# Sigmoid attention and a token MLP: the first q load in two parts, the first three score steps on 256 and 192 queries, group 1's k cast by VectorE

## The chip, the cores and the metric

The kernel runs on one core of a Trainium2 chip. The core has five engines with a queue each, worked in order: TensorE (PE; its weight loads are shown apart as PEld), VectorE (DVE), ScalarE (ACT), GpSimd (POOL) and SyncE (SP), which here issues loads and stores. The transfers themselves run on 16 DMA engines. Matmul results land in PSUM, eight banks of 128 x 512 float32; all else is in SBUF. The metric is the device time of one execution in microseconds (us), lower being better.

## The reference

For 8 batches (u), 12 heads, 448 tokens and 64 values per head, all in float32:

```python
scores = scale * np.matmul(q, k.transpose(0, 1, 3, 2)) - np.log(S)
attn = 1.0 / (1.0 + np.exp(-scores))
x = np.matmul(attn, v)              # then heads side by side: (8, 448, 768)
wq, wk = x @ w_q, x @ w_k           # 768 -> 64
W_tok = scale * np.einsum('bsd,btd->bst', wq, wk)
mixed = np.einsum('bst,btd->bsd', W_tok, x)
out = np.maximum(mixed, 0.0) @ w_out
```

The attention is a sigmoid, so there is no row maximum and no sum to wait for: each block of scores becomes weights by one activation.

## The kernel before, in words

**Groups.** Four heads of one batch are a group; there are 24 groups (u, j). A group's q, k and v come as one load each of 128 x 896 float32 (`load1`, L165): partitions hold two heads by 64 rows, the free dimension holds the other two heads (g) by seven token blocks (i) by 64 values. Each is cast to bf16 (`cast1`, L188; GpSimd unless named otherwise).

**Transposes.** Scores need q and k with the head's 64 values on partitions. For groups 0 to 3, TensorE transposes all of q and k of a group into one PSUM pair (two banks), and one copy moves both to the tile `qk` (`tr`, L267 and L272). Group 4 and many later ones are cast into another layout (L178) and transposed by VectorE (L242, L218).

**Steps.** A group has seven score steps, one for each block of 64 keys (`scores`). A step takes a PSUM pair, makes four 64 x 64 matmuls of all 448 queries (L284), and ScalarE turns 128 x 896 scores to bf16 weights with the sigmoid (L289). Its pair is free when that activation is done. Steps are counted through: step 7 is the first of group 1, step 24 the fourth of group 3. `values` (L302) multiplies the weights with v; after seven steps the sum is copied to `xt` (L311). Then follow transposes of x (L325, L342), the MLP's matmuls (L368, L412, L452 and others) and the output projection (L497, L577), whose results are stored.

**What sets the order.** The string `PLAN` gives the order of the work on TensorE, one letter per piece: S a score step, q and k the transposes of the next group, P or p a values step, F a filler matmul of zeros, K (before only) the second part of group 0's k, other letters the rest. Other engines follow, since their instructions are emitted with the piece that needs them. PSUM pairs are handed out in turn from a list of four, `free2`. A filler writes to the pair that is next in that list. `ORDER` gives the order of loads; a point marks a cast by VectorE. The tiles `ld` for loads are six, so `pump_loads` issues a load once the tile six places before has been cast: SP waits for that cast. `cast_one` lets VectorE's casts be emitted `LAG` = 9 steps after their load.

**The start.** q of group 0 is loaded whole (L637), k in two parts (blocks 0 to 2, L638; 3 to 6, L639). During the first loads TensorE makes 32 matmuls of zeros (L650). VectorE casts blocks 0 to 3 of q, ScalarE 4 to 6, GpSimd both parts of k (L747). `tr_part` transposes one part into a pair and copies it to `qk[0]` (L758): q by VectorE and ScalarE, k by VectorE. Steps 0 and 1 follow, then the second k part, steps 2 to 4, group 1's q transposes, step 5, its k transposes, step 6, step 7. The end of `qk[1]`'s copy (L272) lets step 7 begin.

Of the kernel before, what the change touches and what calls it, by code (L numbers as in the profile page):

```python
# [10 lines left out]
BF16 = mybir.dt.bfloat16  # L11
# [6 lines left out]
def kernel(  # L18
# [12 lines left out]
    nc = tc.nc  # L31
# [4 lines left out]
    P = 128  # L36
# [35 lines left out]
    def bank2():  # L72
        n = free2.pop(0)
        return n, pairs[n], pairs16[n]
# [35 lines left out]
    def xt(u, j):  # L110
# [4 lines left out]


    PLAN = (
        "FFSSFKSFSSqFSkFSFSpFSpSqpPpPSPSSkFSpPSFSSabSrPSPSPXSsPSPpPSp"
        "pPpSPSXSwwSSzWWXwWSPPpSPppNSPSqkSXSSpUSPSpMpSPpPSqkSSPSpPMSP"
        "PPPSSWWXSSwWWWSPpcPSdMpSPPPSXSNSxSqkSUSpPSMppSppPSOoSMSOOqSk"  # L120
        "SoOSMrPpSppPSPSPOoSSsSOzXOSCLlLSLSLLSpPPPPcpPSSdOOSOSCNxSOSc"
        "USPPSPdprPSPPSPPsPPPSpSOPSXoSxSzooSCMLlCSLllLSPcpPSPPPPSCSOd"
        "XSSOOoSMpcpSPPPPSPSONSMYOxSpPpSpSCoodSpPPSoOSxSUSLcldllSLLPS"
        "PpSPpcpPdSoSOMSoSOSXmMrPsSpPPSPoSpOSPoSoozxSoScOSSOOOSOdNSOS"
        "USPppSMPpppPPPSpLPlSLLeppSflLOomgcOMooNOSxSoOStoSSOooeSpPdPP"
        "oPSpSPooSOfSooSSgPOoMpppSPPPOmMOSOSOSLLLlLSLSOoSOxScoOxSoSOO"
        "NdPPSPPPPSSPoOSOSOSooSxoSOSTPpSPPSPppPPMPPypMpPlLMLLyLLIxiiN"
        "IIuiIMiImmIIIOooOOOOoOOoooooo"
    )
    PLAN = "".join(PLAN)  # L130
    KIND = ["a"] + [t for t in PLAN if t in "qacer"]
# [102 lines left out]
    def tr(n, nm, kind):  # L234
        t = "qk".index(nm)
        if kind == "s":
            return
        if kind == "r":
            qk[n] = p_qk.tile([P, 2, 2, NI, NP], BF16, tag="qk", name="qk")
            w = pq[n].rearrange("p e t i d y -> p e (t i d y)").bitcast(F32)  # L240
            for e in range(2):
                nc.vector.transpose(out=qk[n][:, e].rearrange("p t i n -> p (t i n)").bitcast(F32), in_=w[:, e])  # L242
# [12 lines left out]
        t16 = ld.pop((nm + "16", n))  # L255
        if t == 0:
            ps_qk[n] = bank2()
        fb, _, ps = ps_qk[n]
        if kind in "abh":
            transposes_whole(ps[:, t], t16, slice(0, NI))  # L260
        else:
            transposes(ps[:, :, t * S : (t + 1) * S], t16, slice(0, NI))
        if t == 1:
            qk[n] = p_qk.tile([P, 2, 2, NI, NP], BF16, tag="qk", name="qk")
            copy = COPY["s" if kind in "jh" else "v"]
            if kind in "abh":
                copy(  # L267
                    out=qk[n].rearrange("p h t i n -> p t i h n"),
                    in_=ps[:, :, 0 : 2 * S].rearrange("p t (i h n) -> p t i h n", i=NI, h=2),
                )  # L270
            else:
                copy(  # L272
                    out=qk[n].rearrange("p h t i n -> p t h (i n)"),
                    in_=ps[:, :, 0 : 2 * S].rearrange("p h (t x) -> p t h x", t=2),
                )
            release(fb)

    ats = {}

    def scores(n, i):  # L280
        fb, sc, _ = bank2()
# [373 lines left out]


    ORDER = (
# [71 lines left out]

    def cast_one(e):  # L730
        todo = BY[e]
        if not (todo and todo[0] in issued and done["S"] >= issued[todo[0]] + LAG and ready(*todo[0])):
# [8 lines left out]
        while cast_one("s") or cast_one("v"):  # L741
            pass

    q016 = p_c16.tile([P, NI, 2, HD], BF16, tag="q16", name="q16")
    k016 = p_c16.tile([P, NI, 2, HD], BF16, tag="k16", name="k16")
    for t16, t32, r, e in ((q016, q0, IA, "v"), (q016, q0, IB, "s"), (k016, k0, KA, "g"), (k016, k0, KB, "g")):
        COPY[e](  # L747
            out=t16[:, r].rearrange("p i b d -> p b i d"),
            in_=t32[:, :, cols(r)].rearrange("p b (i d) -> p b i d", d=HD),
        )  # L750
    cast |= {("q", 0), ("k", 0)}
    pump_loads()
    qk[0] = p_qk.tile([P, 2, 2, NI, NP], BF16, tag="qk", name="qk")

    def tr_part(nm, t16, r, e):
        fb, _, ps = bank2()
        transposes_whole(ps[:, 0], t16, r)
        COPY[e](  # L758
            out=qk[0][:, :, "qk".index(nm), r].rearrange("p h i n -> p i h n"),
            in_=ps[:, 0, 0 : (r.stop - r.start) * P].rearrange("p (i h n) -> p i h n", h=2, n=NP),  # L760
        )
        release(fb)

    tr_part("q", q016, IA, "v")
    tr_part("q", q016, IB, "s")
    tr_part("k", k016, KA, "v")
# [7 lines left out]
    for t in PLAN:  # L774
# [29 lines left out]
        elif t == "z":  # L804
# [1 line left out]
            quadrants(n, 1)  # L806
            used.update({("q", n), ("k", n)})
            pump()
        elif t == "K":
            tr_part("k", k016, KB, "v")  # L810
        elif kind == "x":
            tr_x(c, tail, t in "XY", "s" if t in "yY" else "v")
        elif kind == "W":
# [58 lines left out]
```

## Time and profile before

| | |
|---|---|
| runs timed | 188.56, 190.07, 192.9 us (median 190.07) |
| the profiled execution | 188.87 us, of which the span of the trace is 186.8 us |
| granted TensorE clock, mean over the span | 0.996 |
| first sigmoid activation starts | 6.36 us |
| step 7's activation (first of group 1) starts | 12.90 us |
| ScalarE busy, 12 to 30 us | 17.96 of 18.00 us |
| TensorE busy, 12 to 30 us, by the model of the trace | 15.62 of 18.00 us |
| DMA engines' mean busy share, 12 to 30 us | 0.96, at 328 GB/s |

All times in the profile count from the start of the span. The profile is of one execution; the timed runs aren't profiled. A line of it names an engine, a source line of the kernel, an operation and the tiles (written <- read); "idle before <- releaser" tells how long the engine stood still and what ended that. Matmul ends are modelled, so that a busy TensorE isn't TensorE at its peak.

### The profile page before, as it was taken

How to read it: one execution, taken by the hardware profiler on the slowest of the kernel's cores; microseconds unless marked ns; L12 is line 12 of the kernel's file. 1: busy time of each engine (PE TensorE's matmuls, PEld its weight loads, DVE VectorE, ACT ScalarE, POOL GpSimd, SP SyncE). 2: the span in 40 equal slices, each digit the busy share in tenths (PEclk: the TensorE clock that was granted, in tenths of full speed). 3: DMA queues.
4: the chain of work that ended last, by engine and by line, in shares of the span. 5: the costliest groups of instructions: out<-in, count | busy, mean ns of one | idle time of the engine just before them, and what ended most of it. 6: DMA issues, size and time to landing. Idle time of an engine off the chain costs nothing.

```text
span 186.8 us, 8517 instructions
## 1 busy us (share of the span) xinstructions
PE 175.1 (94%) x3653; PEld 115.8 (62%) x3656; DVE 139.1 (74%) x211; ACT 163.8 (88%) x210; POOL 107.5 (58%) x145
## 2 busy tenths in 40 slices
PE   7778899989999999999999999999999999999990
PEld 7234556554555554565555776767998889786670
DVE  3234597677878999989898999979768565797810
ACT  4799999999999989999999999998999989975130
POOL 1454886894979989899999885387023820010000
PEclk9999999999999999999999999999999999999998
DMA  5998999985699989999999996994799733603485
GB/s 170 345 375 297 274 373 375 386 307 191 186 344 402 402 296 332 295 321 301 258 260 321 317 408 237 266 321 118 207 346 320 184 93 88 160 19 85 102 238 169
DMA packets 26389, 48.97 MB, mean 262 GB/s; under 512 B 4080, under 2 KB 20208, under 8 KB 26352
## 3 DMA queue, kind: packets, MB, share of 16 engines
q1 hardware_dynamic: 25952, 47.65, 78.2%
q10 hardware_dynamic: 400, 0.79, 1.2%
q8 instruction: 28, 0.46, 1.0%
q14 instruction: 9, 0.07, 0.1%
HBM read 35.78 MB, written 11.01 MB: 251 GB/s over the span
## 4 chain that ended last, share of the span: by engine, by line
PE 66%; DVE 14%; DMA 8%; ACT 4%; issue 3%; POOL 2%; SPq 1%; ACTq 0%; DVEq 0%; POOLq 0%
PE banks L284 14%; PE banks L302 13%; PE banks L497 13%; PE banks L577 10%; DMA q<-in_q_dram 4%; DVE qk L218 4%; DMA k<-in_k_dram 4%; DVE xt L311 3%; PE banks L534 3%; ACT at L289 3%; PE banks L368 3%; PE banks L412 3%; PE banks L342 2%; DVE mx L440 2%; PE banks L325 2%
## 5 line engine op out<-in xcount | busy, mean ns | idle before, releaser
L289 ACT ACTIVATE at<-banks 128x896 bf16<-128x896 f32 x168 | 141.8, 927 | 4.8 <-PE banks L284 3.4
L284 PE MATMUL banks<-qk 64*64 64x448 bf16 x672 | 62.8, 359 | 3.5 <-DVE qk L272 0.9
L302 PE MATMUL banks<-at,v 64*64 64x448 bf16 x672 | 46.6, 350 | 0.2
L284 PEld LDWEIGHTS <-qk 64*64 64x64 bf16 x672 | 25.8, 105 | 24.6 <-issue 14.2
L497 PE MATMUL banks<-wout,mx 64*64 64x384 bf16 x672 | 35.1, 323 | 0.0
L188 POOL CAST v<-v 128x896 bf16<-128x896 f32 x22 | 20.4, 931 | 17.6 <-DMA v<-in_v_dram 14.0
L302 PEld LDWEIGHTS <-v 64*64 64x64 bf16 x672 | 23.1, 106 | 7.8 <-issue 1.7
L497 PEld LDWEIGHTS <-mx 64*64 64x64 bf16 x672 | 24.2, 107 | 3.5
L440 DVE TENSOR_SCALAR mx<-banks 128x1024 bf16<-128x1024 f32 (+2 forms) x21 | 21.1, 1010 | 5.3 <-PE banks L464 3.0
L311 DVE CAST xt<-banks 128x896 bf16<-128x896 f32 x20 | 21.6, 1083 | 4.5 <-PE banks L302 2.6
L577 PE MATMUL banks<-wout,mx 128*128 128x384 bf16 (+1 forms) x138 | 24.7, 320 | 0.0
L577 PEld LDWEIGHTS <-mx 128*128 128x128 bf16 x138 | 11.9, 98 | 10.4 <-issue 4.5
L178 POOL CAST qk<-q 128x896 bf16<-128x896 f32 x13 | 15.5, 1196 | 2.7 <-DMA q<-in_q_dram 1.3
L178 POOL CAST qk<-k 128x896 bf16<-128x896 f32 x11 | 13.4, 1217 | 6.4 <-DVE qk L249 5.2
L249 DVE STREAM_TRANSPOSE qk<-qk 128x448 f32<-128x448 f32 x24 | 14.9, 629 | 0.0
L377 POOL COPY wq<-wqk 64x448 bf16<-64x448 bf16 x6 | 3.7, 619 | 16.9 <-DVE wqk L376 16.6
L153 POOL COPY qk<-swap 32x448 uint32<-32x448 uint32 x20 | 11.9, 593 | 1.2
L147 POOL COPY swap<-qk 32x448 uint32<-32x448 uint32 x20 | 11.1, 554 | 1.8 <-DVE qk L178 0.7
L506 DVE COPY o<-banks 128x768 f32<-128x768 f32 x9 | 8.6, 953 | 4.6 <-PE banks L497 4.6
L150 POOL COPY qk<-qk 32x448 uint32<-32x448 uint32 x20 | 11.1, 554 | 1.2
L606 ACT COPY o<-banks 128x384 f32<-128x384 f32 x10 | 4.8, 485 | 7.1 <-PE banks L577 4.9
L218 DVE STREAM_TRANSPOSE qk<-qk 32x448 f32<-32x448 f32 x16 | 10.2, 636 | 0.4
(91 smaller groups left out, 228.4 us busy)
## 6 DMA issues: line engine op xcount, KB each, us to landing
q<-in_q_dram SPq DMA_DIRECT2D x24, 448.0 KB, 6.2
v<-in_v_dram SPq DMA_DIRECT2D x24, 448.0 KB, 6.4
k<-in_k_dram SPq DMA_DIRECT2D x23, 448.0 KB, 6.1
out_dram<-o SPq DMA_DIRECT2D x51, 192.0 KB, 4.1
w<-in_moe_w_out_dram SPq DMA_DIRECT2D x6, 384.0 KB, 4.8
wout<-wout SPq DMA_DIRECT2D x12, 96.0 KB, 5.6
out_dram<-o ACTq DMA_DIRECT2D x3, 192.0 KB, 3.2
qk<-mv SPq DMA_DIRECT2D x8, 56.0 KB, 3.0
```

The costliest lines, as they stand in the source:

```text
L153: eng.tensor_copy(out=w[lo, 1], in_=z[lo])
L178: COPY[e](out=f[:, :, "qk".index(nm)].rearrange("p e i d y -> p e y i d"), in_=ld.pop((nm, n)).rearrange("p (y i e d) -> p e y i d", y=2, ...
L188: COPY[e](out=t16.rearrange("p i b d -> p b i d"), in_=ld.pop((nm, n)).rearrange("p b (i d) -> p b i d", i=NI),)
L218: nc.vector.transpose(out=qk[n][other : other + 32, h].rearrange("p t i n -> p (t i n)").bitcast(F32), in_=w[own : own + 32, 1 - h],)
L249: nc.vector.transpose(out=qk[n][:, t].rearrange("p t i n -> p (t i n)").bitcast(F32), in_=w)
L284: nc.tensor.matmul(sc[HALF[h], g, 0:S], qk[n][HALF[g], h, 1, i, :], qk[n][HALF[g], h, 0].rearrange("p i n -> p (i n)"), start=True, stop=True,
L289: nc.scalar.activation(at, sc[:, :, 0:S], ACTF.Sigmoid, bias=attn_bias, scale=attn_scale)
L302: nc.tensor.matmul(ps[HALF[g], h, 0:S], ld["v16", n][HALF[h], i, g, :], ats[n, i][HALF[h], g, :], start=(i == 0), stop=(i == NI - 1),)
L311: COPY[eng](out=xt(u, j)[:, :, 0:S], in_=ps[:, :, 0:S])
L440: nc.vector.tensor_scalar(dst, ps, moe_scale, 0.0, ALU.mult, ALU.max)
L497: nc.tensor.matmul(ps[HALF[x], y, 0:NB], mx[HALF[y], u, b, 64 * (i - 3 * y) : 64 * (i - 3 * y) + 64], wout16[HALF[y], slot(y, b), x * NB : ...
L577: nc.tensor.matmul(ps, mxs[w][:, 2 * S * c + m * P : 2 * S * c + (m + 1) * P], wout16[:, c, w0:w1], start=(c == 0), stop=(c == NC - 1),)
```

## The change

1. q of group 0 is loaded in two parts: blocks 0 to 3, then (behind k's first part) blocks 4 to 6.
2. Casts and transposes of group 0 are cut finer: q in three parts (0-1 VectorE, 2-3 ScalarE, 4-6 VectorE), k in four (block 0 and 1-2 GpSimd, 3-4 VectorE, 5-6 GpSimd). The copies of ScalarE's q part stay with ScalarE, all others go to VectorE.
3. Steps 0 to 2 are each done in two parts, 256 queries and then 192 (`scores_part`), with an activation for each part. All three keep their PSUM pair until the second part is done.
4. 23 matmuls of zeros come first, not 32, and three small fillers of 128 columns stand between the parts (`filler`).
5. Group 1's k is cast by VectorE (the point ahead of `k1` in `ORDER`, and no `LAG` for it), and its q and k are copied out of PSUM one by one, each as soon as it is transposed.
6. `PLAN` begins after step 2: step 6 stands ahead of group 1's k transposes, where it was behind them. The rest is as it was.

```diff
     PLAN = (
-        "FFSSFKSFSSqFSkFSFSpFSpSqpPpPSPSSkFSpPSFSSabSrPSPSPXSsPSPpPSp"
+        "FSSqFSFSkFSpFSpSqpPpPSPSSkFSpPSFSSabSrPSPSPXSsPSPpPSppPpSPSX"
...
@@ tr
+        if n == 1:
+            if t == 0:
+                qk[n] = p_qk.tile([P, 2, 2, NI, NP], BF16, tag="qk", name="qk")
+            nc.vector.tensor_copy(
+                out=qk[n][:, :, t].rearrange("p h i n -> p h (i n)"), in_=ps[:, :, t * S : (t + 1) * S],
+            )
+            if t == 1:
+                release(fb)
+            return
...
+    sc0 = {}
+
+    def scores_part(i, r):
+        if i not in sc0:
+            sc0[i] = bank2(), p_at.tile([P, 2, S], BF16, tag="at", name="at")
+        (fb, sc, _), at = sc0[i]
+        c = slice(r.start * NP, r.stop * NP)
+        for g in range(2):
+            for h in range(2):
+                nc.tensor.matmul(
+                    sc[HALF[h], g, c], qk[0][HALF[g], h, 1, i, :],
+                    qk[0][HALF[g], h, 0, r].rearrange("p i n -> p (i n)"), start=True, stop=True,
+                )
+        nc.scalar.activation(at[:, :, c], sc[:, :, c], ACTF.Sigmoid, bias=attn_bias, scale=attn_scale)
+        if r.stop == NI:
+            release(fb)
+            ats[0, i] = at
...
+    PARTS = dict(
+        q=((slice(0, 2), "v"), (slice(2, 4), "s"), (IB, "v")),
+        k=((slice(0, 1), "g"), (slice(1, 3), "g"), (slice(3, 5), "v"), (slice(5, 7), "g")),
+    )
...
-    nc.sync.dma_start(out=q0, in_=src["q"])
-    nc.sync.dma_start(out=k0[:, :, cols(KA)], in_=src["k"][:, :, cols(KA)])
-    nc.sync.dma_start(out=k0[:, :, cols(KB)], in_=src["k"][:, :, cols(KB)])
+    for nm, t, r in (("q", q0, IA), ("k", k0, KA), ("q", q0, IB), ("k", k0, KB)):
+        eng = nc.sync
+        eng.dma_start(out=t[:, :, cols(r)], in_=src[nm][:, :, cols(r)])
...
-    for _ in range(32):
+    for _ in range(23):
...
-        "q1 k1 v0 q2 .k2 v1 k3 q3 q4 k4 v2 w0 v3 k5 k6 q5 "
+        "q1 .k1 v0 q2 .k2 v1 k3 q3 q4 k4 v2 w0 v3 k5 k6 q5 "
...
+    for nm, x in (("q", 0), ("q", 1), ("k", 0), ("k", 1)):
+        cast_part(nm, x)
+    tr_part("q", 0)
+    tr_part("q", 1)
+    tr_part("k", 0)
+    filler()
+    tr_part("k", 1)
+    filler()
+    scores_part(0, IA)
+    cast_part("q", 2)
+    scores_part(1, IA)
+    scores_part(2, IA)
+    tr_part("q", 2)
+    cast_part("k", 2)
+    cast_part("k", 3)
+    cast |= {("q", 0), ("k", 0)}
+    pump_loads()
+    filler()
+    for i in range(3):
+        scores_part(i, IB)
+    tr_part("k", 2)
+    tr_part("k", 3)
     used |= {("q", 0), ("k", 0)}
+    done["S"] = 3
     pump()
```

`cast_part` and the new `tr_part` are the old casts (L747) and copies (L758) for one part of that table; `filler` is one matmul of zeros, 128 columns, into the pair next in `free2`.

More of the change, by code (lines that the diff above doesn't have):

```diff
@@ L117 @@
     PLAN = (
-        "FFSSFKSFSSqFSkFSFSpFSpSqpPpPSPSSkFSpPSFSSabSrPSPSPXSsPSPpPSp"
[L119 to L128, printed above, removed]
+        "FSSqFSFSkFSpFSpSqpPpPSPSSkFSpPSFSSabSrPSPSPXSsPSPpPSppPpSPSX"
+        "SwwSSzWWXwWSPPpSPppNSPSqkSXSSpUSPSpMpSPpPSqkSSPSpPMSPPPPSSWW"
+        "XSSwWWWSPpcPSdMpSPPPSXSNSxSqkSUSpPSMppSppPSOoSMSOOqSkSoOSMrP"
+        "pSppPSPSPOoSSsSOzXOSCLlLSLSLLSpPPPPcpPSSdOOSOSCNxSOScUSPPSPd"
+        "prPSPPSPPsPPPSpSOPSXoSxSzooSCMLlCSLllLSPcpPSPPPPSCSOdXSSOOoS"
+        "MpcpSPPPPSPSONSMYOxSpPpSpSCoodSpPPSoOSxSUSLcldllSLLPSPpSPpcp"
+        "PdSoSOMSoSOSXmMrPsSpPPSPoSpOSPoSoozxSoScOSSOOOSOdNSOSUSPppSM"
+        "PpppPPPSpLPlSLLeppSflLOomgcOMooNOSxSoOStoSSOooeSpPdPPoPSpSPo"
+        "oSOfSooSSgPOoMpppSPPPOmMOSOSOSLLLlLSLSOoSOxScoOxSoSOONdPPSPP"
+        "PPSSPoOSOSOSooSxoSOSTPpSPPSPppPPMPPypMpPlLMLLyLLIxiiNIIuiIMi"
+        "ImmIIIOooOOOOoOOoooooo"
     )
@@ L731, in cast_one @@
         todo = BY[e]
-        if not (todo and todo[0] in issued and done["S"] >= issued[todo[0]] + LAG and ready(*todo[0])):
+        if not (todo and todo[0] in issued and done["S"] >= issued[todo[0]] + (LAG if todo[0][1] > 1 else 0) and ready(*todo[0])):
             return False
@@ L742, in cast_by_others, with cast_part, tr_part @@
             pass
-    q016 = p_c16.tile([P, NI, 2, HD], BF16, tag="q16", name="q16")
-    k016 = p_c16.tile([P, NI, 2, HD], BF16, tag="k16", name="k16")
-    for t16, t32, r, e in ((q016, q0, IA, "v"), (q016, q0, IB, "s"), (k016, k0, KA, "g"), (k016, k0, KB, "g")):
+    t16s = {nm: p_c16.tile([P, NI, 2, HD], BF16, tag=nm + "16", name=nm + "16") for nm in "qk"}
+    t32s = dict(q=q0, k=k0)
+    pump_loads()
+    def cast_part(nm, x):
+        r, e = PARTS[nm][x]
         COPY[e](
-            out=t16[:, r].rearrange("p i b d -> p b i d"),
-            in_=t32[:, :, cols(r)].rearrange("p b (i d) -> p b i d", d=HD),
-        )
-    cast |= {("q", 0), ("k", 0)}
-    pump_loads()
+            out=t16s[nm][:, r].rearrange("p i b d -> p b i d"),
+            in_=t32s[nm][:, :, cols(r)].rearrange("p b (i d) -> p b i d", d=HD),
+        )
     qk[0] = p_qk.tile([P, 2, 2, NI, NP], BF16, tag="qk", name="qk")
-    def tr_part(nm, t16, r, e):
+    def tr_part(nm, x):
+        r, e = PARTS[nm][x]
         fb, _, ps = bank2()
-        transposes_whole(ps[:, 0], t16, r)
-        COPY[e](
+        transposes_whole(ps[:, 0], t16s[nm], r)
+        COPY["s" if e == "s" else "v"](
             out=qk[0][:, :, "qk".index(nm), r].rearrange("p h i n -> p i h n"),
@@ L762, in tr_part, with filler @@
         release(fb)
-    tr_part("q", q016, IA, "v")
-    tr_part("q", q016, IB, "s")
-    tr_part("k", k016, KA, "v")
+    def filler():
+        nc.tensor.matmul(pairs[free2[0]][:, 0, 0:P], zeros[:, 0:P], zeros[:, 0:P], start=True, stop=True)
+    for nm, x in (("q", 0), ("q", 1), ("k", 0), ("k", 1)):
[14 more added lines that the diff above has]
+    cast |= {("q", 0), ("k", 0)}
+    pump_loads()
+    filler()
[3 more added lines that the diff above has]
+    tr_part("k", 3)
     used |= {("q", 0), ("k", 0)}
+    done["S"] = 3
     pump()
@@ L808 @@
             pump()
-        elif t == "K":
-            tr_part("k", k016, KB, "v")
         elif kind == "x":
```

## The prediction

> **What bounds the kernel now.** I read three things in this order: the busy times, ScalarE's instructions in order of time, and the chain that ended last up to 30 us. The page's first row:
>
> ```profile
> PE 175.1 (94%) x3653; PEld 115.8 (62%) x3656; DVE 139.1 (74%) x211; ACT 163.8 (88%) x210; POOL 107.5 (58%) x145
> ```
>
> TensorE's 94% is modelled, so the place matters more than the share. ScalarE, which applies the sigmoid (L289, 168 times), in order of time (start, length, instructions merged, then the idle time before and its releaser):
>
> ```profile
> 4.02 0.51 ACT L747 CAST q<-q 128x384 bf16<-128x384 f32 x1 [1.79 <-DMA q<-in_q_dram]
> 5.11 0.48 ACT L758 COPY qk<-banks 128x384 bf16<-128x384 bf16 x1 [0.57 <-PE banks L210]
> 6.36 5.17 ACT L289 ACTIVATE at<-banks 128x896 bf16<-128x896 f32 x6 [0.78 <-PE banks L284]
> 11.94 43.90 ACT L289 ACTIVATE at<-banks 128x896 bf16<-128x896 f32 x53 [0.40 <-PE banks L284]
> 55.77 0.48 ACT L606 COPY o<-banks 128x384 f32<-128x384 f32 x1
> 56.16 1.73 ACT L289 ACTIVATE at<-banks 128x896 bf16<-128x896 f32 x2
> ```
>
> From 11.94 on it has no gap for 43.9 us. So every tenth gained before 11.94 looks like a tenth of the whole. The chain of waits says otherwise: it doesn't pass through ScalarE there, but through loads. Its first pieces (start, length, what):
>
> ```profile
> 2.76 7.04 DMA k<-in_k_dram
> 9.85 0.93 POOL k L188
> 11.02 0.94 POOL v L188
> 11.98 7.54 DMA q<-in_q_dram
> 19.57 2.33 POOL qk L178 x2
> 21.93 1.07 DVE qk L242 x2
> ...
> 25.08 1.10 DVE xt L311
> 26.22 0.38 PE banks L284 x4
> ```
>
> The load of q for group 4 ends at 19.52, GpSimd casts q and k of that group, VectorE works without a gap from 21.93 to 26.18, and only then does a PSUM pair come free for the scores step that TensorE starts at 26.22. That step is the 25th (number 24, counting from 0): its matmuls end at 26.61, its sigmoid starts at 26.72. Two limits of nearly the same length lie side by side, then: ScalarE's stream and the loads. Is the second one a matter of bytes or of issue? GpSimd's casts show it:
>
> ```profile
> 12.27 0.93 POOL L188 CAST q<-q 128x896 bf16<-128x896 f32 x1 [0.32 <-DMA q<-in_q_dram]
> 16.13 0.93 POOL L188 CAST v<-v 128x896 bf16<-128x896 f32 x1 [2.93 <-DMA v<-in_v_dram]
> 17.42 0.93 POOL L188 CAST k<-k 128x896 bf16<-128x896 f32 x1 [0.35 <-DMA k<-in_k_dram]
> 19.57 1.19 POOL L178 CAST qk<-q 128x896 bf16<-128x896 f32 x1 [0.18 <-DMA q<-in_q_dram]
> ```
>
> GpSimd waits for data each time, and the 16 DMA engines are busy 102% of 6.36 to 12.00 and 96% of 12 to 30 (packets overlap a little). The queue is full; issuing earlier brings nothing.
>
> **The change part by part.**
>
> *q in two loads.* The trace's typical packets are 74 ns for 1792 B, 46 for 1024, 37 for 768; each engine has 16 per load. The first part (1024 B) so lands 16 x 28 ns = 0.45 us before the whole q did (4.00): 3.55. The first k part, behind it, moves from 4.52 to 4.07. All of q costs an engine 16 x (46+37-74) = 0.14 us more. SP issues one load more, 0.50 us by the starts 0.74, 1.24, 1.74; the four loads behind it are issued that much later. The full queue hides this: q of group 2, issued at 3.78, lands at 12.12. Without that cover it would cost 0.5.
>
> *First activation.* Casts of smaller width by the straight line through rows of the same engine: ScalarE 384 columns 0.51, 896 0.93, so 256 about 0.38 to 0.41; GpSimd 384 0.50 and 512 0.61, so 128 0.28 and 256 0.39. q: 3.55 + 0.05 + 0.41 cast + 0.05 + 0.28 (two transposes: 0.22 + 0.06) + 0.05 + 0.38 copy = 4.77. k: 4.07 + 0.05 + 0.28 + 0.39 = 4.79, two transposes and a filler to 5.2, though step 0 needs the first k block only, since TensorE works in order. Scores of 256 columns: 0.37 - 192/448 x 0.19 (two sets of four take 0.57, one 0.38) = 0.29, so the first activation at about 5.5 against 6.36.
>
> *Six small activations for three.* Start to start a full one takes 0.81, one of 384 columns 0.39 (55.77 to 56.16); 512 lies between 0.39 and 0.81, by the line at 0.50. A pair costs 0.89, so three pairs cost 0.24 more (0 to 0.6). What comes late next is the second q part. The third load of before (k's second part) landed at 6.71, though the second did at 4.52. In that place the q part, shorter by 16 x 9 ns and 0.45 us further ahead, lands at 6.1; were the engines even, at 4.7. I take 6.1, the row of that place. Cast 0.36, transposes 0.33, copy 0.36, scores 0.26 and hand-overs: the second parts start at 7.7, with ScalarE idle from 7.0, and end at 8.9. Step 3 waits behind the k transposes, which use step 0's PSUM pair, and a filler on step 1's: about 9.2, against 9.00 before (8.5 if even). So the head start is gone by then.
>
> *Group 1's k by VectorE, q and k copied singly.* Before, step 6 stood on TensorE behind the k transposes and started at 11.94, 0.54 after ScalarE could have; now it stands ahead of them. k lands at 9.80; VectorE casts such a tile in 0.63 (its row: 627 ns) against 0.93. Transposes 0.41. The copy of both took 1.09; one alone is bounded by 0.54 (half) and 0.69 (1024 columns), I take 0.62. The wait for k now stands in VectorE's queue, ahead of the two copies of this group and nothing that is due sooner; q's copy goes first (10.5 to 11.1), k's ends at 11.8, step 7 can start on ScalarE at 12.2. The stream from step 3 reaches it at 9.2 + 4 x 0.81 = 12.45; before it was 12.90. **Gain there: 0.45 us** (0.2 to 0.75). GpSimd loses a cast of 0.93, but v, next in its queue, lands only at 10.96, so nothing behind it moves.
>
> *The rest of the way.* The order behind step 7 is the same. Transposes of group 3's q, at 19.61, waited 0.20 for ScalarE; their cast ends at 19.39 and doesn't move, so 0.2 is left there. At step 24 VectorE still starts from group 4's k, cast until 21.89, and works without a gap until 26.18. With matmuls until 26.61 the sigmoid can start at 26.66: 0.06 is left, and the 0.14 of extra packets goes against it. From there on TensorE's and VectorE's work is what it was.
>
> *Sum.* The execution that was profiled took 188.87 (span 186.8, 2.1 around it). The sum is 188.87 + 0.14 - 0.06, by the unknowns down to -0.2, that is, **no change: 188.8**. The timed runs were 188.56, 190.07 and 192.9, so the profiled one is 1.2 below their median; for a median I take the middle between both, 189.5, less 0.1: 189.4.
>
> **The rivals.**
>
> 1. *The gain passes through.* The last engine's lag decides. From group 2's q (12.12) to the v behind k (16.07) two loads took 3.95 us where later ones come every 1.15: one engine fell 1.6 us back. If it falls back less in the changed run, loads are off the path and ScalarE's 0.45 to 0.75 stays: 188.1 to 188.4, or 188.8 on the scale of the median. For it: ScalarE's 43.9 us without a gap. Against: GpSimd's waits for loads. It decides from 0.5 us less lag on.
>
> 2. *Slower: TensorE stays at its low clock.* The 128-column warm-up matmuls take 314 ns, the transposes of the same width from 4.50 on 219, so the clock rises about 4.4, after 3.4 us of unbroken work. The change issues 23 of them instead of 32, at 3.59/32 = 0.11 each: work stops at 3.5 and resumes at 3.9. If the clock then rises only past 9 us, TensorE's 3.9 us of work between 6.36 and 12.00 (5.64 us) grows towards 7, steps 3 to 7 come up to 1.2 late, which takes the gain of 0.45 and 0.7 more; ScalarE has no idle time to win it back: 189.6, 190.2 on the median's scale. Against it: the gap is only 0.4 us, and TensorE kept its clock over the gap of 0.93 at 6.5. [...]
>
> 3. *Slower: the laggard falls back further.* The same lag of 1.6 us, met once more by smaller packets, moves group 4's k, and with it step 24, by as much: up to 190.4, 191.0 on the median's scale.
>
> 4. *It doesn't do what it says:* the first q part lands no sooner than the whole, because the start of the stream is slow whatever its size. The first activation is then at 5.9; the end is the forecast's, since loads decide.
>
> **Chances.** Forecast and the fourth together 0.55, first 0.22, second 0.10, third 0.13. The range reaches from the lowest run with the full gain (188.56 - 0.75, 187.8) to the median with the third rival's loss (190.07 + 1.3, 191.4). None of the cases reaches 2% (3.8 us), which is about what a measurement of this kernel can tell from no change, with runs 4.3 us apart; what I leave outside is that scatter and the unforeseen: faster 0.03, within 0.91, slower 0.06.
>
> **What would show it.** First activation near 5.5; a gap on ScalarE before the second parts, ended by the second q part's load; step 7 near 12.45 with no gap at step 6; then new idle time of ScalarE or TensorE near 19.5 and 26, with group 4's casts again at 19.6 and 20.7. The forecast is wrong if these casts start half a microsecond earlier or later, or if matmuls behind 4.5 us still take over 300 ns at 128 columns.

## The result, and the profile after

| | before | after |
|---|---|---|
| runs timed (median, lowest to highest) | 189.53 us (188.56 to 192.9, 6 runs) | 192.47 us (190.71 to 194.08, 6 runs) |
| the profiled execution, its span | 188.87, 186.8 us | 190.71, 188.9 us |
| first sigmoid activation | 6.36 us | 5.71 us |
| step 3's activation | 9.00 us | 10.02 us |
| step 7's activation (first of group 1) | 12.90 us | 14.25 us |
| last step's activation (step 167) | 162.03 us | 164.33 us |

The ratio is 1.0147, 95% interval 1.0103 to 1.0192: 2.0 to 3.6 us slower, where I had forecast no change, and the median of 192.47 lies above my range (187.8 to 191.4). The ratio is below the 2% that I took as the bound of a change, but its interval lies wholly above 1. Ratios, here and below, leave out executions that took over 1.5% longer than the fastest of the same kernel. The profiled pair lies 1.8 us apart, and the profiled execution of the kernel after is the fastest of its six.

The busy times hide it. The page's first row of the kernel after:

```profile
PE 178.1 (94%) x3659; PEld 116.0 (61%) x3659; DVE 141.4 (75%) x218; ACT 164.1 (87%) x213; POOL 106.8 (57%) x145
```

TensorE has 3.0 us more of busy time for six instructions more: the same matmuls take longer. Where that begins is seen in ScalarE's instructions in order of time, kernel after (start, length, instructions merged, idle time before and its releaser):

```profile
5.71 1.58 ACT L302 ACTIVATE at<-banks 128x512 bf16<-128x512 f32 x3 [0.77 <-PE banks L298]
7.94 1.25 ACT L302 ACTIVATE at<-banks 128x384 bf16<-128x384 f32 x3 [0.65 <-PE banks L298]
10.02 3.77 ACT L316 ACTIVATE at<-banks 128x896 bf16<-128x896 f32 x4 [0.82 <-PE banks L311]
14.25 3.36 ACT L316 ACTIVATE at<-banks 128x896 bf16<-128x896 f32 x4 [0.46 <-PE banks L311]
```

The head start is there (5.71), and at step 3 it has become a delay of 1.02. Each gap is ended by TensorE. The four steps 3 to 6 take 3.77 us of ScalarE, though they need 0.81 each. TensorE in order of time, the same kernel:

```profile
3.10 0.53 PE L681 MATMUL banks<-zeros 128*128 128x128 bf16 x3
3.92 0.61 PE L210 MATMUL banks<-ident,q 128*128 128x128 bf16 x4 [0.29 <-DVE q L781]
...
4.98 0.31 PE L799 MATMUL banks<-zeros 128*128 128x128 bf16 x1
...
8.86 0.59 PE L833 MATMUL banks<-zeros 128*128 128x512 bf16 x1
9.38 0.96 PE L311 MATMUL banks<-qk 64*64 64x448 bf16 x8
...
11.18 0.59 PE L311 MATMUL banks<-qk 64*64 64x448 bf16 x4
11.70 0.61 PE L833 MATMUL banks<-zeros 128*128 128x512 bf16 x1
12.24 0.57 PE L311 MATMUL banks<-qk 64*64 64x448 bf16 x4
...
12.97 0.39 PE L833 MATMUL banks<-zeros 128*128 128x512 bf16 x1
```

and the kernel before, same view:

```profile
9.62 0.39 PE L776 MATMUL banks<-zeros 128*128 128x512 bf16 x1
9.94 0.38 PE L284 MATMUL banks<-qk 64*64 64x448 bf16 x4
```

The filler of 512 columns is a gauge: 0.59 to 0.61 us at 8.86 and 11.70, 0.39 at 12.97, and 0.39 already at 9.62 in the kernel before. Four score matmuls tell the same: 0.59 at 11.18, against 0.38 at 9.94 before. The trace's records of the granted clock put the rise at 12.67 us in the kernel after and at 4.47 in the kernel before. From there the granted value stays at 1 for 174.08 and 180.91 us, which is 51 and 53 times 3.413; a stretch of 3.41 us is called a window below. (The profile's clock column reads 1.00 ahead of the first record, so a late first rise is seen by durations alone.) Up to there TensorE works at about half speed (in e1 below, where the record says 0.50, the same four matmuls take 0.59 as well), and it has no gap from 7.51 on, so every piece of it is on the path. The chain of waits of the kernel after says the same. It comes to step 7 through nothing but TensorE and one copy:

```profile
12.31 0.51 PE banks L311 x4
12.81 0.29 PE banks L202 x25
13.13 0.64 DVE qk L266
13.77 0.04 issue
13.81 0.41 PE banks L311 x4
14.25 0.85 ACT at L316
```

In the kernel before this chain ran through loads there. From step 7 on the delay of 1.35 us stays what it is, step for step, up to step 72; later jumps bring it to 2.30 by step 167.

A second thing differs. SyncE's DMA issues in order of time, kernel after:

```profile
4.29 1.02 SPq L165 DMA_DIRECT2D q<-in_q_dram  x1
9.45 0.37 SPq L165 DMA_DIRECT2D k<-in_k_dram  x1
11.80 0.37 SPq L165 DMA_DIRECT2D v<-in_v_dram  x1
12.28 0.51 SPq L165 DMA_DIRECT2D k<-in_k_dram  x1
```

The ninth issue, k of group 2, leaves at 9.45 (7.40 before, where it is the eighth), the next, group 1's v, at 11.80 (7.88 before). The first of these moments is the end of GpSimd's cast of group 1's q (8.49 to 9.42), the second the end of its cast of group 0's v (10.84 to 11.78). SyncE's waits before them are released by these two casts, too. So the two loads seem to have got these tiles' buffers. In the kernel before the first waited for the cast of group 0's k (6.76 to 7.37), and the second left right behind it. That a load waits for the tile six places before it, as I said of the kernel before, fits neither: by that rule the two would wait for the casts of group 0's q and k. The DMA engines run dry. Bytes per time from 9 to 15 us in 40 slices, after and then before:

```profile
GB/s 406 418 418 394 394 370 370 359 323 323 335 323 299 239 227 372 299 382 346 346 239 143 131 96 36 96 167 143 108 143 227 191 263 370 418 394 394 394 406 430
```

```profile
GB/s 359 406 418 394 382 382 382 335 311 287 358 370 346 335 370 371 370 394 382 430 406 382 382 406 382 370 406 394 406 406 444 323 347 335 335 394 382 394 418 406
```

In this execution it cost nothing that the steps show, since the late clock came first: the delay is 1.35 at steps 17 and 24 as at step 7, and GpSimd's waits for data stay short, kernel after:

```profile
18.82 0.93 POOL L188 CAST q<-q 128x896 bf16<-128x896 f32 x1 [0.64 <-DMA q<-in_q_dram]
20.03 1.18 POOL L178 CAST qk<-q 128x896 bf16<-128x896 f32 x1 [0.27 <-DMA q<-in_q_dram]
```

### The profile page after: what moved, and what is told of

Read it like the earlier page. It is cut to its first block, busy times and chain, and to the rows that moved or that the text cites. A ratio compares the mean times of both kernels' runs of the same rounds, so it can differ in the third digit from the quotient of the medians.

```text
span 188.9 us, 8539 instructions
## 1 busy us (share of the span) xinstructions
PE 178.1 (94%) x3659; PEld 116.0 (61%) x3659; DVE 141.4 (75%) x218; ACT 164.1 (87%) x213; POOL 106.8 (57%) x145
## 4 chain that ended last, share of the span: by engine, by line
PE 70%; DVE 12%; ACT 6%; DMA 5%; issue 3%; SPq 0%; ACTq 0%; DVEq 0%
PE banks L311 16%; PE banks L524 13%; PE banks L329 12%; PE banks L604 10%; ACT at L316 6%; PE banks L561 3%; DVE xt L338 3%; DMA out_dram<-o 3%; DVE qk L218 3%; PE banks L395 3%; PE banks L439 2%; DMA q<-in_q_dram 2%; PE banks L369 2%; PE banks L352 2%; PE banks L479 1%
## 5 line engine op out<-in xcount | busy, mean ns | idle before, releaser
L316 ACT ACTIVATE at<-banks 128x896 bf16<-128x896 f32 x165 | 139.4, 927 | 5.9 <-PE banks L311 4.1
L404 POOL COPY wq<-wqk 64x448 bf16<-64x448 bf16 x6 | 4.2, 694 | 19.2 <-DVE wqk L403 18.9
L153 POOL COPY qk<-swap 32x448 uint32<-32x448 uint32 x20 | 11.4, 569 | 1.2
```

The costliest lines, as they stand in the source:

```text
L316: nc.scalar.activation(at, sc[:, :, 0:S], ACTF.Sigmoid, bias=attn_bias, scale=attn_scale)
```

## The experiments

Three theories stood against each other: **the clock** (the change breaks TensorE's unbroken work at the start, and the clock rises late), **the loads** (they are issued later), and **the two parts** (more and smaller instructions cost more than the early start gives). Sixteen kernels ran. "Rise" is the first rise of the granted clock in the profiled execution; then the start of the activations of steps 0, 3 and 7; "end" is how much later than in the kernel before step 167 starts. Ratios are to the kernel before on the same chip, with 95% intervals.

| kernel | ratio | rise | step 0 | step 3 | step 7 | end |
|---|---|---|---|---|---|---|
| before | 1 | 4.47 | 6.36 | 9.00 | 12.90 | 0 |
| after | 1.0147 [1.0103, 1.0192] | 12.67 | 5.71 | 10.02 | 14.25 | +2.30 |
| e1: after, 32 warm-ups | 1.0100 [1.0058, 1.0143] | 3.90 | 5.46 | 9.16 | 12.36 | +3.12 |
| e2: before, 23 warm-ups | 1.0019 [0.9987, 1.0051] | 9.90 | 7.33 | 10.17 | 13.37 | +0.66 |
| e3: after, 27 warm-ups, 3 small fillers | 1.0078 [1.0032, 1.0125] | 4.04 | 5.50 | 9.71 | 13.32 | +3.77 |
| e4: before, group 1's part, cast early | 1.0060 [1.0024, 1.0097] | 6.19 | 6.86 | 10.22 | 13.43 | +0.73 |
| e5: e3, 8 load buffers | none | 3.88 | 5.58 | 10.10 | 13.49 | +1.06 |
| e6: after, 8 load buffers | 1.0152 [1.0059, 1.0244] | 13.61 | 5.76 | 10.05 | 14.41 | +4.76 |
| e7: before, 8 load buffers | 1.0019 [0.9971, 1.0066] | 5.57 | 6.67 | 9.08 | 13.37 | +1.71 |
| e8: before, group 1's part | 1.0029 [0.9980, 1.0079] | 5.51 | 6.66 | 9.09 | 12.43 | +2.05 |
| e9: after, 27 warm-ups, 3 small and 6 wide fillers, 8 load buffers | 1.0079 [1.0039, 1.0119] | 3.88 | 5.62 | 9.84 | 13.88 | +1.67 |
| e10: e8, 8 load buffers | 0.9981 [0.9950, 1.0012] | 6.17 | 6.93 | 9.34 | 12.53 | +0.46 |
| e12: e9 with 6 load buffers | 1.0134 [1.0079, 1.0189] | 4.29 | 5.47 | 9.56 | 12.77 | +4.85 |
| f1: after, 32 warm-ups, 8 load buffers | 1.0057 [1.0012, 1.0101] | 3.83 | 5.55 | 9.64 | 12.96 | +2.86 |
| f2: f1, steps 0 to 2 whole | 1.0158 [1.0094, 1.0223] | 13.42 | 7.90 | 10.83 | 15.03 | +2.28 |
| f4: e10, q in two loads | 1.0115 [1.0064, 1.0165] | 4.19 | 8.55 | 11.34 | 14.54 | +4.29 |

e11 and f3 ran once each (below). For e5 only two executions count (189.37 and 190.33), too few for an interval. All columns but the ratio are one execution each. "End" holds stops of 0.5 to 1.7 us late in the run that came in every family, so the ratios judge a kernel and the columns to step 7 explain it.

### The clock: e1 and e2

e1 gives the changed kernel the 32 matmuls of zeros again, e2 takes nine of them from the kernel before.

```diff
-    for _ in range(23):
+    for _ in range(32):
```

> The changed kernel with 32 warm-up matmuls again, not 23. Clock theory (the missing nine let TensorE fall idle near 3.5 us, so that its clock rises at 12.7 instead of 4.5 us): 128-column transposes take 219 ns from 4.5 us on, the first activation is near 6.1 (the warm-up now holds the transposes until 4.5), step 7 starts between 12.2 and 12.7 instead of 14.25, and the time is 0.994 to 1.001 of the kernel before. Split theory (the two-part steps and the late second q part cost the time by themselves): step 7 stays at 13.5 or later, 1.007 or more. Load theory (the loads of k and v for groups 2 and 1 that are issued at 9.5 and 11.8 instead of 7.4 and 7.9 cost it): these issues stay late, the time stays at 1.010 to 1.019.

> The kernel before with 23 warm-up matmuls instead of 32 and nothing else. Clock theory: the clock rises a window or more later, past 7 us, step 7 starts 0.7 to 1.5 us later than 12.90, and the time is 1.004 to 1.014 of before. Split theory and load theory: nothing moves, 0.997 to 1.003, since neither the steps nor the loads change.

In e1 the clock rose at 3.90, and the start went as I had forecast: first activation at 5.46, step 3 at 9.16 (forecast 9.2), step 7 at 12.36 (forecast 12.45). So the clock is what broke that part, in the executions that were profiled. But the loss stayed (1.0100 and 1.0147 have intervals that overlap), since the late loads now showed. GpSimd, TensorE and ScalarE of e1 in order of time:

```profile
19.64 0.93 POOL L188 CAST q<-q 128x896 bf16<-128x896 f32 x1 [2.37 <-DMA q<-in_q_dram]
20.63 0.65 PE L210 MATMUL banks<-ident,q 128*128 128x128 bf16 x7 [1.63 <-POOL q L188]
21.95 0.59 PE L311 MATMUL banks<-qk 64*64 64x448 bf16 x4
22.66 1.73 ACT L316 ACTIVATE at<-banks 128x896 bf16<-128x896 f32 x2 [1.90 <-PE banks L311]
```

Group 3's q, issued at 12.39, landed at 19.51 (10.81 and 18.41 before); step 17 lost 2.03 us. Behind TensorE's idle time the clock fell for one window (0.50 from 20.97 to 24.38), so that the slower transposes are part of these 2.03. Busy times of e1 (start:end, length, busy time and count of TensorE, its weight loads, VectorE, ScalarE, GpSimd, then the granted clock, DMA share and GB/s):

```profile
16.00:20.97 4.97, 3.05 (x64) 1.38 (x60) 1.28 (x2) 4.76 (x6) 2.23 (x4) 1.00 1.01 344
20.97:24.38 3.41, 3.41 (x36) 1.86 (x34) 2.17 (x3) 1.72 (x3) 2.99 (x3) 0.50 1.02 258
```

e2 had the late clock as well (9.90), and step 7 was 0.47 late for it, yet its time is that of the kernel before within half a per cent. Step 3 was 1.17 late, and by step 7 most of that was gone. From 4.49 on TensorE of e2 has no gap, so that the 3.41 us up to its rise at 9.90 were full. In the kernel after a wait of 0.45 for the copy of q's second part, up to 7.31, lies in the window that ended at 9.26, counted back from its rise, and the clock rose one window later. So nine warm-ups fewer are nearly free in the kernel before; that the second q part is what makes them dear in the kernel after is read from these two traces, not tested apart.

### Fillers, and the buffers for loads: e3, e5, e6, e7, e9, e12

e3 puts 27 warm-ups and three small fillers more between the first transposes. e9 and e12 add six fillers of 512 columns that wait for nothing, into a bank that nobody reads. Eight buffers for loads:

```diff
-    p_ld = pool("ld", 6)
+    p_ld = pool("ld", 8)
```

> The changed kernel with 27 warm-up matmuls, up to the arrival of the first q part, and three more small fillers between the first transposes, so that TensorE is never idle up to 5 us. Clock theory: full clock near 4.5, first activation at 5.5 to 5.7, step 3 at 8.5 to 9.3, step 7 at 12.0 to 12.5, the time 0.993 to 0.999 of before. If the change is slow for another reason: step 7 past 13.5 and 1.007 or more.

> The changed kernel with the warm-up and fillers of e3_after_fill and, besides, eight load buffers instead of six, so that the loads of k for group 2 and v for group 1 wait for no cast. Load theory (the change makes these two loads wait for the casts of group 1's q and group 0's v, 9.0 and 11.4 us, the DMA engines run short of work near 12 us, and group 3's q comes too late for step 17): both are issued before 7 us, group 3's q lands by 18.4 (19.5 in e1 and e3), step 17 waits for no cast, and the time falls from 1.008 to between 0.994 and 1.000 of the kernel before. Clock theory alone: no change against e3, 1.003 to 1.012.

> The changed kernel with eight load buffers and nothing else, its 23 warm-up matmuls kept. Load theory: the late loads are gone, the late clock stays: 1.002 to 1.010 (the changed kernel: 1.015). Clock theory alone: 1.010 to 1.019. If the two add up, this and e3 should both lie below the changed kernel, and their gains together give e5.

> The kernel before with eight load buffers and nothing else, as a control: in it the same two loads are issued at 7.4 and 7.9 us and the DMA engines are busy without a break, so all theories expect 0.997 to 1.003. A time below that would mean that e5 and e6 gain by the buffers for another reason than the late loads.

> The changed kernel with 27 warm-up matmuls, three small fillers more between the first transposes, six fillers of 512 columns that wait for nothing (they write to a PSUM bank that no one reads) in TensorE's pauses of steps 0 to 2, and eight load buffers. Both suspects are taken away. If the late or falling clock and the late loads are the whole: clock up near 4 us and not down again before 20 us, step 7 at 12.0 to 12.6, no wait for a cast at step 17, and 0.995 to 1.001 of the kernel before. If a third cost stands behind step 7 (the profiles of the changed kernel, e1, e3, e5 and e6 have pauses of 0.2 to 0.3 us at steps 92, 109 and 145, those of e2, e4, e7 and e8 don't): about 0.6 us more, 0.998 to 1.005, with the pauses there again.

> As e9, with six load buffers. Clock up as in e9, and if the late loads cost by themselves: step 17 waits for group 3's q cast (19.6 us) again, 1.003 to 1.010, above e9. If only the clock counts: as e9.

Read in pairs. e12 and e9 differ by the buffers alone, with a clock that is up by 4.29: step 17 loses 2.39 us in e12 (group 3's q issued at 13.47, landed at 20.10, clock at half speed from 21.36 to 24.77) and nothing in e9, and the ratio goes from 1.0134 to 1.0079. e6 and the kernel after differ by the buffers alone too, with a late clock in both: 1.0152 against 1.0147. The intervals of e12 and e9 overlap, and the two profiled executions lie at opposite ends (193.24 is the slowest of e12's, 189.97 near the fastest of e9's), so the traces carry this reading and not the ratios: the late loads cost where the clock is early, and are hidden where it is late; either repair alone shows the other fault. e7 says that eight buffers by themselves bring the kernel before nothing. Even with both repaired (e9) 0.8% stays. Step 7 comes at 13.88 there, since group 1's q landed at 9.72 (8.43 in the kernel after) and TensorE waited 0.79 us for its cast; with the same fillers step 7 came at 12.77 in e12, so the fillers aren't the cause. In e3 and e5 the clock, though up at 4, fell for one window at 7.3 to 7.5.

### Group 1's part alone: e4, e8, e10

The kernel before, with group 1's k cast by VectorE, its q and k copied one by one, and step 6 ahead of the k transposes. In e4 the cast may be emitted at once, in e8 and e10 after step 3; e10 has eight buffers.

```diff
-        "q1 k1 v0 q2 .k2 v1 k3 q3 q4 k4 v2 w0 v3 k5 k6 q5 "
+        "q1 .k1 v0 q2 .k2 v1 k3 q3 q4 k4 v2 w0 v3 k5 k6 q5 "
...
-        "FFSSFKSFSSqFSkFSFSpFSpSqpPpPSPSSkFSpPSFSSabSrPSPSPXSsPSPpPSp"
+        "FFSSFKSFSSqFSFSkFSpFSpSqpPpPSPSSkFSpPSFSSabSrPSPSPXSsPSPpPSp"
```

> The kernel before with its 32 warm-up matmuls, and of the change only group 1's part: its k cast by VectorE, its q and k copied one by one, step 6 ahead of the k transposes. If everything behind step 7 follows ScalarE (as the even shift of 1.35 us behind step 7 in the changed kernel says): step 6 at 11.4, step 7 at 12.2, the time 0.7 us less, 0.994 to 0.998. If loads set the pace up to step 24, as the prediction had it: step 24 stays at 26.6 to 26.8 and the time at 0.999 to 1.002.

> The kernel before with only group 1's part of the change, once more, with VectorE's cast of k emitted after step 3 as in the changed kernel (in e4 it stood ahead of the copy of group 0's second k part and held up step 3 to 10.2 us). Step 3 at 8.9 to 9.1 when the clock is up by 4.5, step 6 at 11.4, step 7 at 12.2. If the shift at step 7 goes through: 0.995 to 0.999. If it is lost at the loads: 0.999 to 1.002.

> The kernel before with group 1's part of the change as in e8 and eight load buffers, which take away the wait that put group 4's k load at 15.1 us in e8 (13.2 before). If e8 lost its 0.47 us at step 24 to that load: the shift of about -0.45 at step 7 is still there behind step 24, and the time is 0.995 to 0.999. If loads set the pace at step 24 whatever is done: no shift behind it, 0.999 to 1.003.

e4 missed by its own fault. VectorE and ScalarE of e4 in order of time:

```profile
8.77 0.63 DVE L188 CAST k<-k 128x896 bf16<-128x896 f32 x1 [2.55 <-DMA k<-in_k_dram]
9.31 0.42 DVE L767 COPY qk<-banks 128x512 bf16<-128x512 bf16 x1
10.22 2.54 ACT L298 ACTIVATE at<-banks 128x896 bf16<-128x896 f32 x3 [0.82 <-PE banks L293]
```

The cast stood on VectorE ahead of the copy of group 0's second k part, which step 3 waits for, and waited there for its load. With the cast behind that copy, e8 starts step 7 at 12.43: 0.47 earlier, against the 0.45 of the forecast. It loses it at step 24, as the prediction said, but by a load that was issued late: group 4's q landed at 18.11 and its k, issued at 15.13 (13.23 before), at 20.70; GpSimd waited 1.41 us for it. With eight buffers (e10) that k was issued at 11.68 and landed at 18.92, step 24 keeps 0.22, and e10 is the only kernel whose ratio is under 1, by an interval that still holds no change. A caution: executions of the kernel before's start reach step 7 at 12.90, 12.93, 12.96 and 13.37 (before, e11, f3, e7), so that a shift of 0.47 in one execution is no larger than that spread.

e8 also issues k of group 2 and v of group 1 at 7.49 and 7.96, as the kernel before does. So group 1's part alone doesn't make these loads late; which of the finer loads and casts of group 0 does, no run separates.

### The two parts: f1, f2, f4

f1 is the changed kernel with both faults repaired plainly: 32 warm-ups, eight buffers. f2 makes its first three steps whole. f4 puts the load of q in two parts into e10.

```diff
-    scores_part(0, IA)
     cast_part("q", 2)
-    scores_part(1, IA)
-    scores_part(2, IA)
     tr_part("q", 2)
...
-        scores_part(i, IB)
+        scores_part(i, slice(0, NI))
```

> The changed kernel with 32 warm-up matmuls instead of 23 and eight load buffers instead of six, so that neither the late clock nor the late load of group 3's q stands in its way. If the two-part steps pay as I forecast, step 7 starts by 12.5 us (12.90 before), step 17 keeps what step 7 gained, and the ratio is 0.995 to 1.000. If they cost, step 3 starts after 9.2 us, and the ratio is 1.003 to 1.012; of that 0.6 to 0.7 us (0.003) is the pauses at steps 92, 109 and 145.

> The same kernel with steps 0 to 2 on all 448 queries at once, after q's second part; all else of the change stays (q in two loads, k in four casts, group 1's k on VectorE). If the two parts cost, the ratio falls to 0.996 to 1.002 and step 3 starts near 9.0 us; step 0 then starts near 7 us. If the loss lies in the rest of the change, it stays where the run with two-part steps is, within 0.003. ScalarE has three activations fewer, so the pauses of 0.28 us at steps 92 and 145 should be gone if they hang on places in the program.

> The kernel before with group 1's part of the change and eight load buffers (0.998 [0.995, 1.001] without the next edit), and q loaded in two parts, its second part behind k's first; steps 0 to 2 stay whole. Step 0 waits for q's second part (landed near 6.1 us in the changed kernel, q whole at 4.0 before), so step 0 starts at 7.2 to 7.6 us (6.36 before) and step 7 at 12.9 to 13.4: ratio 1.000 to 1.004. If ScalarE can make it up before step 7, the ratio stays at 0.997 to 0.999.

f1 halves the loss and more: 1.0057 against 1.0147, with intervals that just don't meet. But its step 7 starts at 12.96, no earlier than before. ScalarE of f1 in order of time:

```profile
7.97 1.25 ACT L302 ACTIVATE at<-banks 128x384 bf16<-128x384 f32 x3 [0.85 <-PE banks L298]
9.64 6.68 ACT L316 ACTIVATE at<-banks 128x896 bf16<-128x896 f32 x8 [0.41 <-PE banks L311]
```

Step 0 was 0.81 ahead, and all of it went into the wait for the second q part (landed 6.27): its cast, transposes, copy and scores put the second activations at 7.97. A filler waits for a PSUM pair of theirs and holds back step 3's matmuls, so that step 3 starts at 9.64. So in this execution the early start, with a good clock and loads in time, gives nothing at step 7, and the gain of group 1's part is gone with it.

f2 didn't tell two parts from whole steps, because its clock rose at 13.42; without the small matmuls TensorE stood 0.77 us from 5.54 on. f4 is plainer. TensorE and ScalarE of f4 in order of time:

```profile
6.92 0.34 PE L210 MATMUL banks<-ident,q 128*128 128x128 bf16 x3 [2.24 <-ACT q L755]
8.55 7.84 ACT L298 ACTIVATE at<-banks 128x896 bf16<-128x896 f32 x9 [0.78 <-PE banks L293]
```

and its busy times, columns as above:

```profile
4.20:7.60 3.40, 1.16 (x16) 0.75 (x14) 0.56 (x2) 0.82 (x2) 0.50 (x1) 1.00 0.89 296
7.60:11.02 3.42, 3.42 (x24) 1.11 (x26) 1.18 (x3) 2.51 (x4) 1.55 (x2) 0.50 1.05 395
```

q's second part landed at 6.33, TensorE waited 2.24 us, and the clock fell for one window: e10's 0.9981 became 1.0115, worse than I had expected (1.000 to 1.004); I had counted the wait and not the clock. The profiled execution is the slowest of f4's six (190.72 to 193.01 us), so the others may have kept their clock. The load in two parts costs by itself, then: with whole steps behind it, it puts a hole of 2.24 us into TensorE's start. Between the first transposes and step 3 TensorE's gaps are 0.45 us at most in the kernel after and 0.70 in f1, so the small steps seem to fill part of that hole; f2, which should have shown it, lost its clock. They don't win anything over a start without the hole (f1 against before).

### Pauses of 0.28 us: e11, f3

In every kernel with steps in two parts, ScalarE pauses at step 92; ScalarE in order of time, kernel after:

```profile
84.84 2.57 ACT L316 ACTIVATE at<-banks 128x896 bf16<-128x896 f32 x3
87.78 4.20 ACT L316 ACTIVATE at<-banks 128x896 bf16<-128x896 f32 x5 [0.37 <-ACT at L316]
```

Its own earlier activation is named as releaser, so it waited for no other engine. Jumps of 0.23 to 0.28 come at step 109 in six of the eight, and of 0.27 to 0.68 at step 145, these released by TensorE. f2, with three activations fewer than f1, has none of the three. ScalarE's queue (with the instructions for semaphores) is 416 long in the kernel before, 417 in f2 and 420 in the kernel after. e11 and f3 put three and four tiny activations ahead of the kernel before:

```diff
     nc.scalar.activation(warm, zeros[:, 0:1], ACTF.Sigmoid, bias=attn_bias, scale=1.0)
+    nc.scalar.activation(warm, zeros[:, 0:1], ACTF.Sigmoid, bias=attn_bias, scale=1.0)   # 3 times, 4 times
```

> The kernel before with its one-column warm-up activation made four times, so that ScalarE has three instructions more, as in the changed kernel. If the pauses at steps 92, 109 and 145 come from where ScalarE's instructions lie in its program, they appear here as well, 0.2 to 0.3 us each, on those steps. If they come from the changed order of the work, there are none, as in the kernel before.

> The kernel before with four tiny activations more at the start of ScalarE's queue, which makes it as long as the changed kernel's. If the pauses come from places in the program, steps 92 and 145 each start 0.25 to 0.3 us later against the step before them than in the kernel before; if they come from something else in the changed kernel, no such pause shows. The time stays 189 to 191 us either way.

e11 (189.48 us) showed no pause. f3 (191.14 us), ScalarE in order of time:

```profile
83.74 2.57 ACT L289 ACTIVATE at<-banks 128x896 bf16<-128x896 f32 x3
86.68 4.20 ACT L289 ACTIVATE at<-banks 128x896 bf16<-128x896 f32 x5 [0.37 <-ACT at L289]
```

The same idle time of 0.37 at the same step, made by four instructions that do nothing. So the pause at step 92 hangs on the place in the program, as f3 shows. In all nine kernels that have it, step 92's activation is the 192nd instruction that the trace lists for ScalarE; in the nine without, it is the 188th, 189th (f2) or 191st (e11). The place isn't all, since in the kernel before step 94's activation is the 192nd and doesn't pause; which machinery makes it, no run tells. At step 109 f3 had none, and at step 145 a stop of TensorE (0.86, released by nothing that the profile shows) covers what there may have been: these two stay open. Together the three are put at 0.16 + 0.24 + 0.28 = 0.68 us in the kernel after: 0.28 at step 92 less 0.12 won back at the next, 0.24 at step 109, and of the jump of 0.47 at step 145 the 0.28 that e5, e9 and f1 show there (an estimate).

## Why the prediction was wrong

Two steps of it failed. Every term from the first activation to step 7 took TensorE at full clock, with nine warm-ups fewer; the clock rose at 12.67 instead, and step 7 came at 14.25, not 12.45. And the loads behind the first eight were taken to be issued as before; two were 2.05 and 3.92 us later, which cost nothing in the profiled execution of the kernel after but about 2 us where the clock was early (e1, e12). The sign that I had named for being wrong was there: the 128-column filler at 4.98 took 0.31 us.

**First q part and first activation: right.** Forecast 3.55, 4.07 and 6.1 for the three landings; 3.54, 4.05 and 5.92 in the kernel after, 3.65, 4.18 and 6.27 in f1. So rival 4 is out. First activation about 5.5; 5.46 to 5.76 in the kernels with the changed start. A pair of small activations takes 0.49 and 0.38 from start to start, 0.87 against 0.89.

**Rival 2 was what happened, with a chance of 0.10 and too small a price.** I had dismissed it because "the gap is only 0.4 us, and TensorE kept its clock over the gap of 0.93 at 6.5". The second half is no argument: the kernel before, with its clock up, kept it over 0.93, and in the kernel after 0.29 lay in a window that didn't raise it. The first half doesn't help either: the gap came to 0.29 only, and the clock still rose at 12.67. That windows lie ahead of the first rise too is an estimate, by counting back in steps of the 3.41 us that the records show behind it. Counted so, the 23 warm-ups, 0.99 to 3.62, reach 1.19 us into the window that begins at 2.43. Windows of the kernel after, counted back from its rise (columns as above):

```profile
2.43:5.85 3.42, 3.12 (x33) 1.96 (x30) 1.10 (x4) 0.92 (x3) 0.63 (x2) 1.00 0.88 242
5.85:9.26 3.41, 2.80 (x29) 1.14 (x21) 1.50 (x5) 2.69 (x6) 1.31 (x2) 1.00 1.01 362
9.26:12.67 3.41, 3.41 (x51) 1.40 (x54) 1.25 (x2) 2.58 (x3) 1.70 (x3) 1.00 0.87 302
```

The clock didn't rise after 3.12 and 2.80 of 3.41, and rose after 3.41. Yet it rose in f1 after a window that wasn't full:

```profile
0.42:3.83 3.41, 2.85 (x27) 2.85 (x28) 1.22 (x12) 1.64 (x3) 0.52 (x3) 1.00 0.50 144
```

TensorE worked 2.85 us of it; its idle time lay ahead of its first matmul (0.98), and the rest was unbroken. Of the 18 profiled executions eight rose at the end of such a first window (2.69 to 3.30 us of work), the other ten at the end of one that TensorE filled (3.36 to 3.41). Seven windows with a gap inside (2.55 to 3.12 us of work) didn't raise it, nor did first windows with 2.38 or less. So in these executions a gap inside a counted window went with a missed rise; the rule behind it stays open. In the kernel before TensorE works without a gap of 0.1 us from 0.99 to 6.50, and in all seven executions with that start the clock was up by 6.62. I had put the point of decision at 9 us; the clock rose 3.7 us behind that, and the price at step 7 came to 1.35 over the kernel before where I had said 0.7.

**Step 3 at 9.2, step 7 at 12.45: right under an early clock** in e1 (9.16, 12.36), 0.4 to 0.5 us too early against f1 (9.64, 12.96). There the second activations start at 7.97 and not at 7.7, of which 0.17 is the later landing of q's second part, and the filler between them and step 3 adds the rest. The terms were right in kind; the condition that all of them hung on, a clock at full speed, wasn't met.

**"The full queue hides this" failed one load further on.** The four loads that I had charged were issued 0.5 us later, as forecast. The two behind them, of which I had said nothing, were issued 2.05 and 3.92 us later (9.45, 11.80), since the buffers that they got came free later, and the queue that I had called full ran at 36 to 239 GB/s between 12.0 and 13.7 us. In e1 and e12 step 17 lost 2.0 and 2.4 us, the slower clock behind the wait included. What I should have asked of every load that the change moves is which buffer it gets and which cast frees that.

**Step 24: "0.06 is left" held where it was tested.** e8, with six buffers, met the wall that I had described: group 4's k was cast at 20.76, and step 24 started at 26.70. But "issuing earlier brings nothing" was too strong: with that load issued earlier (e10), step 24 came 0.22 sooner, in one execution. A delay passes the wall, as rival 2 had it (+1.35 in the kernel after). The sum itself is off by a little: 188.87 + 0.14 - 0.06 is 188.95, not 188.8.

**Gain of group 1's part: near the forecast at step 7, not seen in the time.** 0.47 and 0.36 (e8, e10) against 0.45, one execution each; the ratios 1.0029 and 0.9981 both hold no change.

**Not foreseen:** the pauses, 0.68 us in the profiled execution.

The sum of the kernel after, by its profile: 1.35 at step 7, 0.68 by the pauses, 0.27 of other jumps, 2.30 by step 167, against 2.1 us of span. The median says 2.9. What the other 0.8 is, no profile shows; single executions of one kernel spread by 2 to 6 us. Repairing clock and loads took the ratio from 1.0147 to 1.0057, each against the kernel before on its own chip: 1.7 us; the pauses account for 0.0036 of the rest, if their sum is taken whole, and what then stays is within the interval of f1.

## What to carry to other kernels

Before a load at the start is cut, look at what keeps TensorE working without a gap: 5.5 us of unbroken work had the clock up by 6.62 us in seven executions of seven, while starts with gaps had it up at 9.90 to 13.61 in four, and up to the rise four score matmuls took 0.59 us where they took 0.38 behind it (e2, f2). For every load behind the cut, find which buffer it gets and which cast frees it; here the buffers didn't come by turn. An early first result is worth only what the last part of the same data lets through.

## What the runs showed of the hardware

- The granted clock rose first at 3.67 to 6.62 us in the seven executions with the kernel before's start (32 warm-ups, q whole), at 3.83 to 4.29 in seven others, and at 9.90, 12.67, 13.42 and 13.61 in four where TensorE had gaps (e2, after, f2, e6). Until the last record it stayed at each value for multiples of 3.41 us: 53 times in the kernel before and 51 times after (180.91 and 174.08 us at 1), once at 0.50 in e1 (20.97 to 24.38).
- Once up, it fell for exactly one window after windows in which TensorE was busy 34, 40 and 45% (f4, e12, e1) and, in e3 and e5, 71 and 68%; in f1, e9 and e4 it stayed up after 67, 60 and 59%. So the busy share alone doesn't tell the two apart.
- TensorE sometimes stops in the middle of a group of four matmuls, with nothing shown that it waits for. TensorE of e8 in order of time:

```profile
118.57 0.35 PE L293 MATMUL banks<-qk 64*64 64x448 bf16 x1
120.16 0.38 PE L293 MATMUL banks<-qk 64*64 64x448 bf16 x3 [1.24 <-issue]
```

Such stops, of 0.5 to 1.7 us by the steps' starts, came between steps 116 and 145 in some executions and not in others, in both families; their cause stays open.
